# An attention and mixture-of-experts kernel: full and small units of the second expert layer share the code of their first tile

## The chip, the cores and the metric

One core of a Trainium2 chip runs the whole kernel. The metric is the device time of one execution in microseconds; the lower the better. All data is float32; products run on float32 values split into a high and a low part.

## The reference, cut to what matters

Three stages follow one another: pooled attention, a first expert layer with one expert, and a second layer with eight experts. Only the second layer is changed:

```python
N, D, E, F = (2304, 512, 8, 1024)
logits = xn @ en.T / tau                 # xn, en: rows scaled to length 1
expert_idx = np.argmax(logits, axis=1)
gate_w = probs[np.arange(N), expert_idx]
for e in range(E):
    mask = expert_idx == e
    if not mask.any():
        continue
    h = np.maximum(x[mask] @ w1[e], 0.0)
    out[mask] = gate_w[mask, None] * (h @ w2[e])
```

Each row of x goes to one expert, so how many rows an expert has is known only at run time.

## The kernel before

The second layer is class `Moe2`. The rows of each expert are cut into units of 256 (two tiles of 128); up to 17 units are in the program, written out one after the other, and from unit 9 on each stands inside a condition that there are that many. With these inputs units 0 to 11 run. A unit whose rows fit in one tile is small: bit u of `half` is set for it, and it takes another path.

For unit u the program first calls `nxt(u + 1)` (L1298): `gather` (L1187) loads the records of the next unit with a DMA from SyncE's queue (L1195), then gathers its rows with two indirect DMAs from GpSimd's queue (L1205) and drains that queue (L1191); then four loads of the next unit's w1 go to SyncE's queue (`load("1")`, L1167; they move data only where the expert changes).

Then comes the branch on `half` (L1320), taken by every engine for itself. The **full** path: `hidden(f)` for f = 0 to 7 (L1226), 12 products of 256 columns each into a PSUM bank, evicted by ScalarE (L1235) and VectorE (L1236) into `hh` and `hl`; beside each, `split("2", f)` splits one eighth of w2 (ScalarE copy L1172, VectorE subtraction L1173). `load("2")` then queues the next w2. `outer(0, f)` for f = 0 to 7 (L1264) is the second product of the first tile, three products of 512 columns for each f (L1269), all in one bank. Behind f = 0 `x_t` (L1220) transposes the next unit's gathered rows (eight transposes, L1212; copies L1216, subtractions L1217), and behind each f `split("1", f)` splits an eighth of the next unit's w1. `store(rec, 0)` (L1273) scales the bank on ScalarE (L1276) and scatters the rows from GpSimd's queue (L1277). `outer(1, f)` and `store(rec, 1)` do the second tile.

The **small** path: `half(x)` (L1238) makes the first product of one tile the other way round, 2 x 12 products of 512 columns (L1247), with the w2 splits between them, evicts each half as `g` (L1252), and `turn(0)`, `turn(1)` (L1255) transpose each half (L1259) and evict it into `hh`, `hl`. Then `outer(0, f)` for the one tile, with `turn(1)` behind f = 1, `x_t` behind f = 5, a w1 split behind each f, and one store. There is no second tile.

All scatters write the same tensor `out`, so a store on GpSimd's queue waits until the one before it has landed. Engines run their instructions in program order; there is no scheduler that would reorder them here. Where a path is not taken, the program raises the counters (semaphores) by what the other path would have raised, so that later waits hold in either case.

Buffers that matter: banks `d_ph` (3), `d_pt` (2), `d_po` (3, one for each call of `po`), gathered rows `d_xg` (4), outgoing rows `d_ob` (4).

Of the kernel before, what the change touches and what calls it, by code (L numbers as in the profile page):

```python
# [1110 lines left out]
class Moe2:  # L1111
# [150 lines left out]
        nc.vector.tensor_sub(out=l, in0=p, in1=h.bitcast(F32))  # L1262

    def outer(self, t, f):  # L1264
        if f == 0:
            self.o = self.po()
        s = slice(t * 128, t * 128 + 128)
        for q, (a, b) in enumerate(((0, "2h"), (0, "2l"), (1, "2h"))):
            self.nc.tensor.matmul(self.o, lhsT=(self.hh, self.hl)[a][f // 4][:, f % 4, s],  # L1269
                                  rhs=self.w[b, f // 2][:, f % 2],  # L1270
                                  start=f == 0 and q == 0, stop=f == 7 and q == 2)
# [9 lines left out]
    def run(self, items):  # L1281

        nc, tc, rt = self.nc, self.tc, self.rt
        evs = []
        rec, x = self.rec0, self.xt0

        def routing():
            while evs:
                evs.pop(0)()
            while items:  # L1290
                f = items.popleft()
                if f is None:
                    return
                e = f()
                if e:
                    evs.append(e)

        def nxt(u):  # L1298
            r = self.gather(u)
            e = nc.sync.value_load(rt.u[0:1, u, 1:2], min_val=0, max_val=E - 1)  # L1300
            c = nc.sync.value_load(rt.u[0:1, u, 2:3], min_val=0, max_val=1)
            self.load("1", e, c)
            return r, e, c

        first = []

        def step():
            if next(steps, None):
                first.extend(nxt(1))

        with ExitStack() as ifs:  # L1311
            for u in range(UMAX):
                if u >= UMIN:
                    ifs.enter_context(tc.If(total > u))
                more = u + 1 < UMAX
                if more and u:
                    (rec1, xs1), e, c = nxt(u + 1)
                if u:
                    x1 = (self.xh(), self.xl()) if more else None
                    with tc.If((half & (1 << u)) == 0) as full:  # L1320
                        for f in range(8):
                            self.hidden(f, x)
                            self.split("2", f)
                        if more:
                            self.load("2", e, c)
                        for f in range(8):
                            self.outer(0, f)
                            if more:
                                if f == 0:
                                    self.x_t(xs1, x1)  # L1330
                                self.split("1", f)
                        self.store(rec, 0)
                        for f in range(8):
                            self.outer(1, f)
                        self.store(rec, 1)
                    with full.Else():
                        self.half(x)
                        if more:
                            self.load("2", e, c)
                        for f in range(8):  # L1340
                            self.outer(0, f)
                            if f == 1:
                                self.turn(1)
                            if more:
                                if f == 5:
                                    self.x_t(xs1, x1)
                                self.split("1", f)
                        self.store(rec, 0)
                    x = x1
                else:  # L1350
                    for f in range(2, 8):
                        self.hidden(f, x)
                        routing()
                        if f == 4:
                            steps = rt.units()
                        for _ in range(min(3, f - 3)):
                            if not first:
                                step()
                        for i in {4: (2, 3), 5: (4, 5), 6: (6, 7)}.get(f, ()):
                            self.split("2", i)  # L1360
                    for f in range(8):
                        self.outer(0, f)
                        step()
                    self.store(rec, 0)
                    self.load("2", *first[1:])
                    for f in range(6):
                        self.outer(1, f)
                        step()
                    while not next(steps, 1):
                        pass  # L1370
                    (rec1, xs1), e, c = first
                    for f in (0, 2, 4, 6):
                        self.split("1", f)
                    x = self.xh(), self.xl()
                    self.x_t(xs1, x, lambda: self.outer(1, 6))
                    self.outer(1, 7)
                    total = nc.values_load(rt.u[0:1, 0, 2:3], min_val=UMIN, max_val=UMAX)
                    half = nc.values_load(rt.half[0:1, 0:1], min_val=0, max_val=(1 << (UMAX + 1)) - 1)
                    for f in (1, 3, 5, 7):
                        self.split("1", f)  # L1380
                    self.store(rec, 1)
                if more:
                    rec = rec1
# [135 lines left out]
```

## Time and profile before

| what | value |
|---|---|
| median of 3 runs | 1192.37 us (1190.85 to 1193.21) |
| profiled execution, its own time | 1190.95 us |
| its span, first to last instruction | 1189.1 us |
| TensorE products busy, share of the span | 1145.3 us, 96% |
| VectorE, ScalarE, GpSimd busy | 882.1, 740.6, 600.4 us |
| mean granted clock of TensorE | 0.987 |
| second layer, unit 1 to the end | from 950.4 us |

The table is an average over three stages; the rows below are of the second layer alone. Times in them are microseconds from the start of the span; "[2.22 <-X]" is idle time of the engine ahead of the row and what by the profile ended it. A TensorE row is drawn to the modelled end of its last product, so it overlaps the next one a little. PEld is the weight load that goes with each product, PEldq its instruction queue (branches, counters).

### The profile page before, as it was taken

To read this page: it belongs to the slowest core of one execution; us is meant where nothing else is said; L and a number is where in the kernel's file an instruction comes from. 1 tells how busy PE (TensorE), PEld (TensorE's weight loads), DVE (VectorE), ACT (ScalarE), POOL (GpSimd) and SP (SyncE) were. 2 spreads that over 40 slices of the span, in tenths; PEclk is the share of its full clock that TensorE was granted. 3 is DMA by queue.
4 is the path that set the end of the run, shared out by engine and by line. 5 is a ranking of instruction groups with operands and counts; after the bars stand their busy time and mean duration, and the time that the engine had idled before them with its cause. 6 is when DMAs were issued, how large, how long until landed. Compare 5 with 4: busy or idle time off the path is not lost. (4 is left out here: it accounts for less than half of the span.)

```text
span 1189.1 us, 21181 instructions
## 1 busy us (share of the span) xinstructions
PE 1145.3 (96%) x7315; PEld 1064.7 (90%) x7315; DVE 882.1 (74%) x1593; ACT 740.6 (62%) x1451; POOL 600.4 (50%) x525
## 2 busy tenths in 40 slices
PE   7999999999999999799789999999999999999997
PEld 6999999999999999689679988998889899887886
DVE  6888898899999998698845674565455776666775
ACT  5888888878788787344334445444435466666664
POOL 6998988877888872698950222012110221121211
PEclk9999999999999999899989999999999999999999
DMA  7787777785869754555314211111222121286443
GB/s 186 176 191 175 173 183 172 167 204 141 208 151 214 169 124 122 162 168 165 123 46 124 72 46 66 55 54 32 78 89 93 46 72 37 77 267 210 141 144 131
DMA packets 87189, 156.14 MB, mean 131 GB/s; under 512 B 26871, under 2 KB 44279, under 8 KB 87056
## 3 DMA queue, kind: packets, MB, share of 16 engines
q1 hardware_dynamic: 82352, 142.34, 44.7%
q0 software_dynamic: 4336, 11.58, 2.9%
q8 instruction: 67, 1.10, 0.4%
q10 hardware_dynamic: 368, 0.59, 0.2%
q14 instruction: 66, 0.54, 0.2%
HBM read 145.84 MB, written 20.08 MB: 140 GB/s over the span
## 5 line engine op out<-in xcount | busy, mean ns | idle before, releaser
L235 DVE TENSOR_SCALAR_CACHE_REDUCE e<-sc 128x1152 f32<-128x1152 f32 x144 | 194.7, 1352 | 23.5 <-PE sc L231 22.2
L242 ACT ACTIVATE e<-e,nm 128x1152 f32<-128x1152 f32 x144 | 183.7, 1276 | 4.8 <-DVE e L235 4.8
L231 PE MATMUL sc<-kT,qt 128*128 128x384 f32 x780 | 159.0, 339 | 9.8 <-DVE e L235 8.2
L269 ACT CAST pth<-pa 128x768 fp32r<-128x768 f32 (+2 forms) x160 | 116.3, 737 | 80.5 <-PE pa L260 80.5
L271 DVE TENSOR_TENSOR ptl<-pa,pth 128x768 fp32r<-128x768 f32 (+2 forms) x160 | 138.9, 876 | 19.9 <-ACT pth L269 7.7
L1173 DVE TENSOR_TENSOR e<-e,e 128x512 fp32r<-128x512 f32 x200 | 129.4, 687 | 30.2 <-ACT e L1172 14.2
L582 DVE SCALAR_TENSOR_TENSOR u<-h,u 128x320 f32<-128x320 f32 (+1 forms) x112 | 55.8, 498 | 128.8 <-ACT u L581 128.2
L578 ACT ACTIVATE u<-h,half 128x320 f32<-128x320 f32 (+1 forms) x112 | 59.8, 534 | 142.7 <-PE h L563 134.3
L231 PEld LDWEIGHTS sc<-kT,qt 128*128 128x128 f32 x780 | 132.2, 188 | 12.3 <-DVE e L235 9.6
L1269 PE MATMUL d_po<-e,e 128*128 128x512 f32 x504 | 120.9, 393 | 0.0
L260 PE MATMUL pa<-idf,e 128*128 128x128 f32 x864 | 117.6, 272 | 1.7 <-DVE ptl L271 1.7
L595 PE MATMUL y<-wh,gl 128*128 128x512 f32 x288 | 113.9, 395 | 0.8 <-POOL gl L586 0.8
L1172 ACT CAST e<-e 128x512 fp32r<-128x512 f32 x200 | 113.7, 619 | 0.7 <-issue 0.3
L595 PE MATMUL y<-wh,gh 128*128 128x512 f32 x288 | 113.9, 395 | 0.0
L595 PE MATMUL y<-wl,gh 128*128 128x512 f32 x288 | 113.6, 394 | 0.0
L1277 POOL DMA_INDIRECT out<-d_ob,d_rec x19 | 22.1, 1162 | 176.9 <-ACT d_ob L1276 120.5
L1269 PEld LDWEIGHTS d_po<-e,e 128*128 128x128 f32 x504 | 92.6, 188 | 18.6 <-DVE e L1173 0.3
L260 PEld LDWEIGHTS pa<-idf,e 128*128 128x128 f32 x864 | 102.9, 140 | 7.0 <-DVE ptl L271 1.3
L563 PE MATMUL h<-xth,wh 128*128 128x320 f32 (+1 forms) x448 | 90.8, 325 | 16.5 <-POOL wh L57 9.5
L584 ACT CAST gh<-u 128x320 fp32r<-128x320 f32 (+1 forms) x112 | 52.4, 468 | 84.9 <-DVE u L582 84.9
L535 POOL TENSOR_TENSOR xl<-xth,xl 128x512 f32<-128x512 f32 (+1 forms) x14 | 18.3, 1306 | 168.6 <-DMA xl<-av_b 139.9
L285 PE MATMUL av<-pth,vh 128*128 128x288 f32 x576 | 103.2, 306 | 0.0
(257 smaller groups left out, 2639.0 us busy)
## 6 DMA issues: line engine op xcount, KB each, us to landing
e<-moe_w SPq DMA_DIRECT2D x104, 512.0 KB
kr<-k SPq DMA_DIRECT2D x63, 288.0 KB
qr<-q SPq DMA_DIRECT2D x62, 288.0 KB
kk<-kT SPq DMA_DIRECT2D x60, 288.0 KB
vr<-v SPq DMA_DIRECT2D x16, 576.0 KB
av_b<-avs SPq DMA_DIRECT2D x64, 128.0 KB
wi<-moe_w_in SPq DMA_DIRECT2D x16, 512.0 KB
wo<-moe_w_out SPq DMA_DIRECT2D x16, 512.0 KB
```

The lines of the kernel that those rows point to most:

```text
L231: nc.tensor.matmul(s[:, j, 0:384], lhsT=a, rhs=b[:, 384 * j:384 * j + 384], start=i == 0, stop=i == len(mm) - 1)
L235: nc.vector.tensor_scalar(out=e.rearrange("p (a b) -> p a b", a=3), in0=s[:, :, 0:384], scalar1=-0.5 / D ** 0.5, scalar2=None, op0=ALU.mul ...
L242: self.nc.scalar.activation(e, e, AF.Exp, bias=d["nm"][:, t:t + 1], scale=-1.0, accum_out=d["sum"][:, t:t + 1])
L260: nc.tensor.transpose(p[:, c // 3, (c % 3) * 128:(c % 3) * 128 + 128], e[:, i * 128:(i + 1) * 128], idf)
L269: nc.scalar.copy(hi, p)
L271: nc.vector.tensor_sub(out=lo, in0=p, in1=hi.bitcast(F32))
L285: nc.tensor.matmul(box["t"][:, 0:GQ], lhsT=self.vh[:, h * 9 + i % 9], rhs=p[:, i % 9, c0:c0 + GQ], start=i == 0, stop=i == 17)
L563: nc.tensor.matmul(ps[:, :n], lhsT=a[:, k], rhs=b[:, k, h0:h0 + n], start=i == 0, stop=i == 11)
L595: self.nc.tensor.matmul(y, lhsT=a, rhs=b, start=j == 0 and q == 0, stop=j == NF - 1 and q == 2)
L1172: self.nc.scalar.copy(hi, r)
L1173: self.nc.vector.tensor_sub(out=lo, in0=r, in1=hi.bitcast(F32))
L1269: self.nc.tensor.matmul(self.o, lhsT=(self.hh, self.hl)[a][f // 4][:, f % 4, s], rhs=self.w[b, f // 2][:, f % 2], start=f == 0 and q == 0, ...
```

## The change

In each unit from 1 on the branch on `half` now holds less. The full path keeps its eight `hidden` and w2 splits, the w2 loads and `outer(0, 0)`, `outer(0, 1)`; the small path keeps `half`, the w2 loads, the same two and `turn(1)`. What follows stands once, for both: `outer(0, 2)` to `outer(0, 7)` with the w1 splits (0 and 1 ahead of f = 2, then f - 1 ahead of each f, 7 at the end), `x_t` ahead of f = 4, and the first store. A second branch on the same bit, without an else path, holds the second tile. The bank of the output is taken outside of the branch, and no longer inside `outer`.

```diff
     def outer(self, t, f):
-        if f == 0:
-            self.o = self.po()
         s = slice(t * 128, t * 128 + 128)
...
                 if u:
                     x1 = (self.xh(), self.xl()) if more else None
+                    self.o = self.po()
                     with tc.If((half & (1 << u)) == 0) as full:
                         for f in range(8):
                             self.hidden(f, x)
                             self.split("2", f)
                         if more:
                             self.load("2", e, c)
-                        for f in range(8):
+                        for f in range(2):
                             self.outer(0, f)
-                            if more:
-                                if f == 0:
-                                    self.x_t(xs1, x1)
-                                self.split("1", f)
-                        self.store(rec, 0)
-                        for f in range(8):
-                            self.outer(1, f)
-                        self.store(rec, 1)
                     with full.Else():
                         self.half(x)
                         if more:
                             self.load("2", e, c)
+                        for f in range(2):
+                            self.outer(0, f)
+                        self.turn(1)
+                    for f in range(2, 8):
+                        if more:
+                            if f == 4:
+                                self.x_t(xs1, x1)
+                            for i in (0, 1) if f == 2 else (f - 1,):
+                                self.split("1", i)
+                        self.outer(0, f)
+                    if more:
+                        self.split("1", 7)
+                    self.store(rec, 0)
+                    with tc.If((half & (1 << u)) == 0):
+                        self.o = self.po()
                         for f in range(8):
-                            self.outer(0, f)
-                            if f == 1:
-                                self.turn(1)
-                            if more:
-                                if f == 5:
-                                    self.x_t(xs1, x1)
-                                self.split("1", f)
-                        self.store(rec, 0)
+                            self.outer(1, f)
+                        self.store(rec, 1)
                     x = x1
```

In unit 0 two calls of `po` are moved out of `outer`, with nothing else changed.

## Rows read from the trace of the kernel before

**Rows 1.** Units 3, 5: length, busy us PE PEld DVE ACT POOL, clock, DMA.

```profile
996.50:1019.60 23.10, 23.10 (x154) 21.16 (x153) 15.04 (x26) 13.76 (x28) 4.34 (x4) 1.00 0.15 48
1042.80:1058.00 15.20, 12.98 (x66) 10.75 (x66) 10.40 (x17) 11.53 (x22) 3.15 (x3) 1.00 0.73 237
```

**Rows 2.** TensorE, units 4 to 6: start, us, line, tiles, count, [idle before].

```profile
1030.96 0.84 PE L1269 MATMUL d_po<-e,e 128*128 128x512 f32 x3
1032.44 10.46 PE L1269 MATMUL d_po<-e,e 128*128 128x512 f32 x45
1045.12 1.16 PE L1247 MATMUL d_ph<-e,d_xh 128*128 128x512 f32 x4 [2.22 <-ACT e L1172]
...
1055.73 1.03 PE L1212 MATMUL d_pt<-idf,d_xg 128*128 128x128 f32 x8
1057.98 0.93 PE L1233 MATMUL d_ph<-d_xh,e 128*128 128x256 f32 x4
```

**Rows 3.** TensorE in order of time, units 7 to 11.

```profile
1083.34 1.32 PE L1247 MATMUL d_ph<-e,d_xh 128*128 128x512 f32 x4 [2.06 <-ACT e L1172]
...
1097.78 0.93 PE L1233 MATMUL d_ph<-d_xh,e 128*128 128x256 f32 x4
...
1121.27 1.08 PE L1247 MATMUL d_ph<-e,d_xh 128*128 128x512 f32 x4
...
1132.97 1.29 PE L1212 MATMUL d_pt<-idf,d_xg 128*128 128x128 f32 x8 [0.98 <-DMA d_xg<-y_rows,d_rec]
...
1135.49 0.87 PE L1233 MATMUL d_ph<-d_xh,e 128*128 128x256 f32 x4
...
1172.24 0.66 PE L1212 MATMUL d_pt<-idf,d_xg 128*128 128x128 f32 x4 [0.85 <-DMA d_xg<-y_rows,d_rec]
```

**Rows 4.** TensorE's branches (L1320), ns min/median/max: at 1039 us, at 1077 us.

```profile
L1320 PEldq COMPARE_BRANCH  x1: 5944/5944/5944, 1039.0 to 1039.0; - x1
L1320 PEldq COMPARE_BRANCH  x2: 315/2946/5576, 1077.1 to 1077.6; - x2
```

**Rows 5.** GpSimd in time: stores, gather (unit 5); gathers (units 7, 9).

```profile
1038.52 1.38 POOL L1277 DMA_INDIRECT out<-d_ob,d_rec  x1 [14.12 <-ACT d_ob L1276]
1047.11 1.00 POOL L1277 DMA_INDIRECT out<-d_ob,d_rec  x1 [7.21 <-DMA out<-d_ob,d_rec]
...
1049.71 1.17 POOL L1205 DMA_INDIRECT d_xg<-y_rows,d_rec  x1 [0.30 <-PE d_pt L1259]
...
1089.31 1.37 POOL L1205 DMA_INDIRECT d_xg<-y_rows,d_rec  x1 [0.30 <-PE d_ph L1247]
...
1128.04 0.97 POOL L1205 DMA_INDIRECT d_xg<-y_rows,d_rec  x1 [0.30 <-issue]
```

**Rows 6.** Issue to landing: store at 1038.52; gathers, units 5, 7, 9.

```profile
DMA to landing us min/median/max: 7.8/7.8/7.8
DMA to landing us min/median/max: 4.0/4.5/5.0
DMA to landing us min/median/max: 3.6/4.1/4.7
DMA to landing us min/median/max: 5.5/5.8/6.2
```

**Rows 7.** ScalarE in order of time, outer products of unit 4.

```profile
1033.24 4.27 ACT L1172 CAST e<-e 128x512 fp32r<-128x512 f32 x8
1037.55 0.69 ACT L1276 ACTIVATE d_ob<-d_po,d_rec 128x512 f32<-128x512 f32 x1
```

**Rows 8.** TensorE: counter step at a skipped block; last products.

```profile
L1311 PEldq EVENT_SEMAPHORE  x1: 51/51/51, 1183.2 to 1183.2; - x1
...
1181.16 1.98 PE L1269 MATMUL d_po<-e,e 128*128 128x512 f32 x8
```

**Rows 9.** TensorE, unit 7: length, busy (instructions), granted clock, DMA share, GB/s.

```profile
1084.20:1087.60 3.40, 3.40 (x10) 0.50 0.55 181
1087.60:1091.00 3.40, 3.40 (x19) 1.00 0.77 264
```

More of the change, by code (lines that the diff above doesn't have):

```diff
@@ L1360, in run @@
                             self.split("2", i)
+                    self.o = self.po()
                     for f in range(8):
@@ L1365, in run @@
                     self.load("2", *first[1:])
+                    self.o = self.po()
                     for f in range(6):
```

## The prediction

> **What bounds the kernel now.** The change touches only the second layer, so I split that by unit. Which units are full and which are small is read from the products: units 1 to 4, 6, 8, 10 and 11 run L1233 (full), units 5, 7 and 9 run L1247 (small); unit 11 is the last one that runs. The first view is the table of stretches: in a full unit TensorE is busy all of its 23.1 us, in a small unit it is not (13.0 of 15.2 us) [rows 1]. Whatever the change brings or costs, it must show as idle TensorE in units 5, 7, 9, or as new idle time in the eight full ones. The second view is TensorE in order of time. There are two kinds of holes. Units 5 and 7 begin with 2.22 and 2.06 us of nothing, unit 9 does not [rows 2, 3]. And the transposes of the next unit's rows wait for their gather: 0.98 us in unit 9 and 0.85 us in unit 11 [rows 3].
>
> The hole at the start of units 5 and 7 is labelled as a wait for a ScalarE copy, but that copy writes w2 parts which the first L1247 products don't read, and w1 was split a unit earlier. The branch instructions explain it: TensorE's branch into the small part took 5944 ns in unit 5 and 5576 ns in unit 7, where the branch at the end of the full part ahead of it took 315 ns [rows 4]. The first started at 1039.0, when the products queued ahead of it still had 3.9 us to run (they end at 1045.12 - 2.22 = 1042.9); the rest is the hole. It looks like code that had to be fetched. The Trainium skill says so ("Runtime: NRT & Kernel Launch", Instruction fetch mechanics): code comes in blocks of 256 instructions, only two are held, and a taken branch to outside of them waits for a fetch. By that rule the trace fits: the full part is 152 products with a weight load each, 304 instructions, so the jump over it can pass a whole block; in the change only 102 products are jumped, 204 instructions, and the target is in this block or the next.
>
> The second chain is GpSimd's queue. The gather for the next unit stands behind the second store of the unit before, which waits until the first store has landed: issued at 1038.52, landed 7.8 us later, so the second store went at 1047.11, and the second gather at 1049.71 [rows 5]. Its rows land 5.0 us after that, at 1054.7; in unit 7 at 1089.31 + 4.7 = 1094.0, in unit 9 at 1128.04 + 5.5 = 1133.5 [rows 5, 6] (the larger of the two numbers is given to the second gather; in unit 9 the other way would fit worse, as the waiting transposes start at 1132.97 [rows 3]). All three lie in stretches where the next expert's weights are loaded.
>
> **The change, part by part.** A product of 512 columns costs 0.23 us (45 in 10.46 us, the last one drawn at full length) [rows 2], the eight transposes of x_t 0.8 us (from 1030.96 + 3 x 0.23 to 1032.44) [rows 2].
>
> Full units: the same products, transposes, splits and stores; no sum on TensorE. x_t moves from behind outer(0, 0) to ahead of outer(0, 4), 9 products or 2.1 us later; its result is first read in the next unit, over 5 us after. ScalarE does three splits of 0.53 us first, then waits for the transposes (1030.96 + 12 x 0.23 + 0.4 = 1034.2), copies until 1035.3, and does five splits until 1038.0; before, it was at 1037.5, with the store at 1037.55 [rows 2, 7]. So the **first store goes 0.5 us later**, and behind it on GpSimd the second store and the gathers. In unit 11 the later x_t finds its rows there: **-0.85 us** [rows 3]. One more taken branch in the middle and one more test: some 0.3 us each in the sequencer [rows 4], hidden by the queued products ahead.
>
> Small units: the hole at the start goes (-2.2, -2.1), the gather does not come sooner, and x_t moves **forward**, from behind outer(0, 5) to ahead of outer(0, 4). In unit 5 x_t began 1055.73 - 1045.12 = 10.6 us after the first product; 6 products fewer lie ahead now, so 9.2 us. It would be due at 1042.9 + 9.2 = 1052.1, in unit 7 at 1081.3 + 9.2 = 1090.5, in unit 9 at 1130.5. The rows land at 1054.7, 1094.0, 1133.5: the saved holes turn into a wait for the gather (a hole that stayed would be over at 1045.1 and x_t due at 1054.3, still ahead of its rows, so the sum hardly hangs on it), and the 6 products that used to run before x_t now stand behind it on TensorE, as do splits 3 to 7 and the store on ScalarE.
>
> A new cost at the end of a small unit: the second tile is a block of its own that is jumped. A jumped block must still raise the counters that its products would have raised; the trace shows such a step once, on TensorE at the end of unit 11: it ran at 1183.2, after the last product's end at 1183.14, and the branch after it took 0.19 us [rows 8]. So TensorE **drains**: product's end 0.16 us past its slot, counter, two branches, test, and a first weight load that nothing covers (about 0.2 us): I take 0.85 us, worked out from these; bounds 0.3 (only the tail of a product) and 1.5.
>
> From the landing on a small unit then needs 0.4 (second transposes) + 12 x 0.23 + 0.85 = 4.0 us. Next unit at 1058.7, 1098.0, 1137.5; before at 1057.98, 1097.78 and 1135.49, with the first four products 0.3 us slow in each (0.93, 0.93, 0.87 for about 0.62) because splits came late, which the drain now covers [rows 2, 3]. Differences: +0.4, -0.1, +1.7, together **+2.0 us**. Later landing: +0.3 per unit of the 0.5 above, **+0.9** (nothing if the store is bound by the loads' bytes anyway, 1.5 at most). In units 5 and 7 the products start 2 us sooner, so two of the w2 loads are issued sooner and stand ahead of the gathers; unit 9, which had no hole, shows the gather at 5.5 us for 5.0 and 4.7: **+0.8 each, 1.6** (0 to 3).
>
> Clock: after the hole of unit 7 the granted clock fell to 0.50 (1.2 GHz) for 3.4 us, in which 10 products ran where 19 run at full clock (2.4 GHz) [rows 9]: 1.7 us. It is inside unit 7's time before. The new waits (2.6, 3.5 and 3.0 us and longer) are longer than that hole, so I count **one such fall in three units, +1.7** (0 to 5.1).
>
> Sum: 2.0 + 0.9 + 1.6 - 0.85 + 1.7 = **+5.3 us**. Against the profiled execution (1190.95, span 1189.1) this is 1196.3; that execution is 1.4 us under the median of the runs shown (1192.37), and I go between the two: **1197**.
>
> **Rivals.** (1) The gathers land as before and the clock stays up: 2.0 - 0.85, about +1.2 us, 1192 to 1193.6. For: the store's landing is set by the four loads issued ahead of it. Against: longer waits than the one that lost the clock. Chance 0.25. (2) **Faster**: the gathers land before x_t is due. Small units then take 9.2 + 0.8 + 2.8 + 0.85 = 13.6 us: units 6, 8 and 10 start at 1056.5, 1094.9 and 1134.9, with the 0.3 -1.8, -3.2 and -0.9, and -0.85 in unit 11: -6.7, some 1185. It decides at a landing 9.2 us after the unit's start, 2.6 to 3.5 us sooner than in the trace. For: it is the landing under load that is slow (7.8 us for the store), and loads could fall otherwise. Against: no issue on GpSimd moves forward. Chance 0.12. (3) Code fetch gets worse: a branch in the middle of each full unit meets missing code. With 6 long and some 12 short products queued ahead (1.4 + 1.3 us) 5.9 us of fetch leaves 3.2, in eight units up to 26 us; 1200 to 1220. The same page of the Trainium skill speaks against further branches in this way; by its block size the jump of some 80 instructions should not leave the two blocks. In the trace the full part's end jump (past the small part's 64 products, 315 ns) never cost a hole. Chance 0.05.
>
> **Numbers.** Forecast 0.58, rivals 0.25, 0.12, 0.05. About 0.2% (2.4 us) is what a measurement can tell from no change. Slower 0.60 (the forecast and rival 3, less the forecast's lowest corner), same 0.27, faster 0.13. The forecast's own range is 1193.5 to 1203 (bounds of landing, drain and clock); with rival 1 from 1191 to 1202.5.
>
> **What would show it.** Right: no TensorE branch over 1 us into units 5, 7, 9 and no hole there; L1212 in those units idle 2.5 to 4.5 us on the gather; an idle stretch of some 0.9 us ahead of units 6, 8 and 10; unit 11 without wait; full units still 23.1 us. Wrong: L1212 of small units without wait (rival 2), holes behind outer(0, 1) of full units (rival 3), or a hole left at the start of unit 5 or 7, which would mean that it was no jump.

## The result, and the profile of the changed kernel

The changed kernel takes 1201.51 us (median), 1.0081 times the kernel before, 95% interval 1.0066 to 1.0096: 9.1 us slower at the medians. One of its five executions took 2100.6 us at a mean granted clock of 0.819; the ratio leaves it out, and without it the median is 1200.61 us. The profiled execution took 1201.92 us with a span of 1200.1, 11.0 us more than the span of before. In this kernel the outer products are L1267, stores L1274 (ScalarE) and L1275 (GpSimd), the first test L1319, the second test L1344 (the two branches on `half`); hidden products L1233, half L1247, turn L1259 and x_t L1212 keep their lines.

TensorE of the changed kernel, units 5 and 6, in order of time (start us, us, engine, line, tiles, shapes, count, in brackets the idle time before and what ended it):

```profile
1041.53 1.08 PE L1247 MATMUL d_ph<-e,d_xh 128*128 128x512 f32 x4
...
1049.20 1.64 PE L1267 MATMUL d_po<-e,e 128*128 128x512 f32 x6
1053.96 0.66 PE L1212 MATMUL d_pt<-idf,d_xg 128*128 128x128 f32 x4 [3.11 <-DMA d_xg<-y_rows,d_rec]
1055.75 1.09 PE L1212 MATMUL d_pt<-idf,d_xg 128*128 128x128 f32 x4 [1.13 <-DMA d_xg<-y_rows,d_rec]
1056.49 5.46 PE L1267 MATMUL d_po<-e,e 128*128 128x512 f32 x12
1062.42 0.73 PE L1233 MATMUL d_ph<-d_xh,e 128*128 128x256 f32 x4 [0.47 <-PEq L1344]
```

The same view, units 7, 9 and 11:

```profile
1085.21 1.08 PE L1247 MATMUL d_ph<-e,d_xh 128*128 128x512 f32 x4
...
1097.35 0.66 PE L1212 MATMUL d_pt<-idf,d_xg 128*128 128x128 f32 x4 [2.82 <-DMA d_xg<-y_rows,d_rec]
1099.37 1.09 PE L1212 MATMUL d_pt<-idf,d_xg 128*128 128x128 f32 x4 [1.37 <-DVE d_xl L1217]
1100.11 4.24 PE L1267 MATMUL d_po<-e,e 128*128 128x512 f32 x12
1104.82 0.73 PE L1233 MATMUL d_ph<-d_xh,e 128*128 128x256 f32 x4 [0.47 <-PEq L1344]
...
1127.61 1.08 PE L1247 MATMUL d_ph<-e,d_xh 128*128 128x512 f32 x4
...
1139.22 0.66 PE L1212 MATMUL d_pt<-idf,d_xg 128*128 128x128 f32 x4 [2.20 <-DMA d_xg<-y_rows,d_rec]
1141.30 1.09 PE L1212 MATMUL d_pt<-idf,d_xg 128*128 128x128 f32 x4 [1.43 <-DVE d_xl L1217]
1142.04 5.36 PE L1267 MATMUL d_po<-e,e 128*128 128x512 f32 x12
1147.95 0.73 PE L1233 MATMUL d_ph<-d_xh,e 128*128 128x256 f32 x4 [0.56 <-PEq L1344]
...
1185.18 1.03 PE L1212 MATMUL d_pt<-idf,d_xg 128*128 128x128 f32 x8
```

Four things are to be read, each against its row of before. The holes (idle time of TensorE) of 2.22 and 2.06 us at the heads of units 5 and 7 [rows 2, 3] are gone. In all three small units x_t now waits, twice: once for each of its two tiles. (The second wait of units 7 and 9 is labelled as a VectorE subtraction; the second gather was issued at 1093.30 and landed 5.9 us later, at 1099.2, which fits the 1099.37 at which the transposes began.) The 12 products behind x_t take 4.2 to 5.5 us, where 0.23 us each would make 2.8. And each small unit ends with half a microsecond in which TensorE's sequencer is at the second test. Unit 11 no longer waits (0.85 us before, [rows 3]).

Why the 12 products are slow is in the table of stretches (length, then busy us and instructions of PE, PEld, DVE, ACT, POOL, then the granted clock, the DMA share and GB/s), taken over the stretches of low clock:

```profile
1054.99:1061.80 6.81, 6.05 (x16) 4.56 (x16) 4.39 (x7) 3.42 (x7) 0.00 (x0) 0.50 0.51 165
1099.37:1102.76 3.39, 3.39 (x10) 2.88 (x11) 1.65 (x3) 2.26 (x5) 0.00 (x0) 0.50 0.00 0
1140.33:1147.13 6.80, 5.83 (x16) 4.56 (x16) 4.39 (x7) 3.34 (x7) 0.00 (x0) 0.50 0.02 5
```

A granted clock of 0.50 (1.2 GHz) stands behind each of the three waits, for 17.0 us in all; before, it was once, for 3.4 us [rows 9].

TensorE's branch at the first test, at the three changes from a full to a small unit (ns min/median/max, then the time):

```profile
L1319 PEldq COMPARE_BRANCH  x1: 218/218/218, 1037.8 to 1037.8; - x1
L1319 PEldq COMPARE_BRANCH  x1: 438/438/438, 1081.5 to 1081.5; - x1
L1319 PEldq COMPARE_BRANCH  x1: 430/430/430, 1124.0 to 1124.0; - x1
```

The 5944 and 5576 ns of before [rows 4] are not there. What the long branches wait for is in the same traces. In the kernel before, one packet of instructions runs on DMA queue 8 from 1040 to 1044 us, inside the branch of 5944 ns (queue, packets, MB, share of 16 engines):

```profile
q8 instruction: 1, 0.02, 1.6%
```

It is 16 KB, runs from 1042.41 to 1043.44 us, and the branch ends 1.5 us behind it. In the 13 traces of this case TensorE has 20 branches of over 1 us; each has one such packet in it, which ends 1.4 to 1.5 us ahead of the branch's end, and no branch of under 1 us into a small unit has one. So the holes are a wait for code, which the prediction could only infer. Last, GpSimd around unit 5 (first store of unit 4, its second store, second gather for unit 6), and the time from issue to landing of that first store and of the gathers:

```profile
1037.66 1.27 POOL L1275 DMA_INDIRECT out<-d_ob,d_rec  x1 [14.43 <-ACT d_ob L1274]
1047.10 1.00 POOL L1275 DMA_INDIRECT out<-d_ob,d_rec  x1 [8.17 <-ACT e L1261]
...
1049.69 0.97 POOL L1205 DMA_INDIRECT d_xg<-y_rows,d_rec  x1 [0.30 <-PE d_pt L1259]
...
DMA to landing us min/median/max: 8.6/8.6/8.6
DMA to landing us min/median/max: 5.5/5.7/5.9
```

The first store goes 3.87 us ahead of the unit's start; before, 4.38 (1038.52 against 1042.90) [rows 5]. It takes 8.6 us to land for 7.8, and the gather 5.9 for 5.0 [rows 6]. So the second gather is issued 8.2 us behind the unit's start for 6.8, and its rows land 14.1 us behind it for 11.8; the transposes of its tile begin at 14.2. Unit 9 is alike (issued at 8.1 for 6.8). In unit 7 the issue is hardly later (8.1 for 8.0), and it is the landing that takes longer, 5.9 us for 4.7 [rows 6].

The whole in one table: lengths of the units in us from the first product of one to the first of the next (the code wait at the head of units 5 and 7, where there is one, is counted to them), and the time at a granted clock of 0.50 ahead of the last product. The rows below the second are the experiments of the next section.

```
kernel                        u5     u6     u7     u8     u9    u10   at 0.50
before                      15.08  23.30  16.50  23.49  14.22  23.32    3.4
changed                     20.89  22.79  19.61  22.79  20.34  23.20   17.0
changed, second profile     19.28  23.20  18.19  22.79  18.02  22.78   10.2
x_t ahead of outer(0, 6)    16.83  22.79  17.93  22.80  14.85  23.22    3.4
x_t behind the first store  14.30  23.78  14.31  23.38  14.40  23.38    0
old branches, x_t forward   17.03  23.63  16.62  23.48  17.91  23.07   10.2
work in the wait            19.90  22.78  17.71  23.20  20.68  22.79    6.8
work at the head            17.08  23.20  16.48  23.20  17.14  22.78    0
gathers between the stores  13.37  23.26  13.37  23.26  13.59  22.79    0
gathers two ahead           13.35  23.30  13.36  22.93  13.60  22.79    0
old branches, two ahead     15.26  23.24  14.96  23.08  13.48  23.08    0
```

Each row is one profiled execution, and not all of these are near their kernel's median: the changed kernel's second profile took 1198.34 us (median 1201.52), x_t behind the first store 1186.22 (1188.14), work at the head 1191.78 (1195.62), old branches with gathers two ahead 1188.41 (1189.72), and work in the wait 1200.32 (1196.23).

In the changed kernel the three small units are 5.8, 3.1 and 6.1 us longer, 15.0 together. The units behind them are 1.3 us shorter, unit 11 1.1 us; the rest of the difference to 11.0 lies ahead of unit 1 (-1.2), in units 1 to 4 (-0.2) and in the last stores (-0.3).

### The profile page after: what moved, and what is told of

It reads as the page before. It is cut to its first block, busy times and chain, and to the rows that moved or that the text cites. A ratio compares the mean times of both kernels' runs of the same rounds, so it can differ in the third digit from the quotient of the medians.

```text
span 1200.1 us, 21374 instructions
## 1 busy us (share of the span) xinstructions
PE 1151.2 (96%) x7315; PEld 1068.8 (89%) x7315; DVE 880.1 (73%) x1593; ACT 739.2 (62%) x1451; POOL 598.6 (50%) x525
## 5 line engine op out<-in xcount | busy, mean ns | idle before, releaser
L1267 PE MATMUL d_po<-e,e 128*128 128x512 f32 x504 | 127.1, 407 | 0.3 <-DVE e L1173 0.3
L1275 POOL DMA_INDIRECT out<-d_ob,d_rec x19 | 21.2, 1118 | 191.2 <-ACT d_ob L1274 126.0
L1267 PEld LDWEIGHTS d_po<-e,e 128*128 128x128 f32 x504 | 96.9, 197 | 20.5 <-DVE e L1173 0.8
```

## The experiments

The theory: a small unit is bound by the landing of the next unit's rows and by what stands behind x_t on TensorE; the branches that the change mends were covered by that wait; the wait then costs more than its length, through the clock. The main rival: the branch structure itself, with its second test, is what costs.

**The changed kernel again**, as a yardstick for the runs beside it.

> The changed kernel once more, unedited, beside the three others of this group, so that they can be compared on one chip. Theory: the loss is a property of the program and not of one execution: 1.008 of the kernel before, about 1201 us, with the waits on the gather in units 5, 7 and 9. Rival: part of the loss was chance in the landings of the first profile, then 1.004 or less, 1196 us.

Measured: 1.0066 (1.0044 to 1.0088), 1201.52 us. The loss is the program's. Its profile, one execution of 1196.6 us span, differs from the first in size: the clock was low for 3.4 us behind each of the three waits, and the transposes of the second gather's rows began 13.9, 13.1 and 12.5 us behind the units' starts, for 14.2, 14.2 and 13.7. Nothing in the program differs, so up to 1.2 us of landing and 1.7 us of clock per unit (half of 6.8 - 3.4) vary from execution to execution.

**x_t later in the new structure.**

```diff
                         if more:
-                            if f == 4:
+                            if f == 6:
                                 self.x_t(xs1, x1)
```

> The changed kernel with one edit: in the shared products x_t stands ahead of outer(0, 6), where the small units had it before the change, not ahead of outer(0, 4). Theory: a small unit is bound by the landing of the next rows (14.2, 14.2 and 13.7 us after its start in the changed kernel) plus everything that stands behind x_t on TensorE. Six products (6 x 0.23 = 1.4 us at full clock, 2.7 at half) move out from behind that wait in each of units 5, 7, 9, so at least 3 x 1.4 = 4.2 us are saved, and up to 11.8 if the granted clock also stays up (units of about 16.5 us in place of 20.9, 19.6, 20.3): 1189.7 to 1197.3 us. Rival: the 9 us come from the branch structure (the second test with its drained TensorE, the branches), and x_t's place is of no matter: 1201 us, as the changed kernel.

Measured: 1.0015 (1.0000 to 1.0030), 1192.98 us. Some 6 to 8 us of the 9 are gone with six products moved, and structure and second test are all still there: the rival falls. The transposes of the second gather's rows still begin 14.3, 14.1 and 12.2 us behind the units' starts, x_t still waits (6.6 us in five waits), but less stands behind it and the clock falls once only.

**The old structure with x_t forward.** The branches of before, x_t ahead of outer(0, 4) in both parts (the small part is shown, the full part is edited alike):

```diff
                         for f in range(8):
+                            if more and f > 1:
+                                if f == 4:
+                                    self.x_t(xs1, x1)
+                                for i in (0, 1) if f == 2 else (f - 1,):
+                                    self.split("1", i)
                             self.outer(0, f)
                             if f == 1:
                                 self.turn(1)
-                            if more:
-                                if f == 5:
-                                    self.x_t(xs1, x1)
-                                self.split("1", f)
+                        if more:
+                            self.split("1", 7)
                         self.store(rec, 0)
```

> The other half of the change alone: the branches of the kernel before (each kind of unit has its products in a part of its own, no second test), but x_t ahead of outer(0, 4) and the splits in the order of the change, in both parts. Theory: x_t's place does most of the harm. The holes at the start of units 5 and 7 come back (2.2 and 2.1 us), but they run beside the gather's way, so the units still end at the landing plus 0.4 + 12 products; no drain (about 0.5 us each). With a clock that falls as in the changed kernel about 1198 to 1201, with less of it 1195. TensorE's branch into units 5 and 7 over 5 us again, and a wait on the gather in all three. Rival: the shared structure is what costs; then this runs as the kernel before, 1192.

Measured: 1.0027 (1.0009 to 1.0046), 1195.33 us. The holes are back (2.82 and 2.16 us, TensorE's branch into unit 5 takes 6544 ns), and as TensorE comes later to x_t, it waits less there (1.1 us at most, 3.1 in the changed kernel). Old branches and late x_t 1, new branches 1.0015, forward x_t 1.0027, both 1.007 to 1.008: the two edits together cost more than their sum. The theory's wording "x_t's place does most of the harm" is thus too strong: x_t forward costs 3 us with the old branches and 6 to 8 with the new, where no hole stands ahead of it. Not all of the 3 us is x_t's: of the 10.2 us at half clock one fall of 3.4 us stands at the hole of unit 5 and one at that of unit 7, the third behind x_t's waits in unit 9, and before had only the one at unit 7 (a fall of 3.4 us costs 1.7 at most). Unit 9 has 0.91 us of idle TensorE behind its first four products, which neither side said; it comes again (0.52 us) in the old kernel below that gathers two units ahead. In both a packet of instructions ends 1.4 and 1.3 us ahead of the product that ends the idle time (1125.54 for 1126.94, 1121.89 for 1123.22), as in the holes. That fits a wait for code behind a short branch; no run tests it.

**Work at the head of a small unit**, where before had its hole.

```diff
                     with full.Else():
+                        p = self.ph()
+                        for j in range(9):
+                            nc.tensor.matmul(p, lhsT=x[0][:, 0, 0:128], rhs=self.w["1h", 0][:, 0],
+                                             start=j == 0, stop=j == 8)
                         self.half(x)
```

> The changed kernel with work added: nine products (2.1 us) at the head of a small unit, into a PSUM tile that nothing reads, in the place of the hole that the kernel before had there. Theory of the prediction: the hole was cover, since the gather's way runs beside it. Then the added 2.1 us come off the wait of x_t (2.0 to 3.1 us) and cost nothing, and as the clock falls for less time the kernel is 3 to 6 us faster than the changed one: 1195 to 1198 us. If, besides, the w2 loads that stand ahead of the gathers in the changed kernel (the term of 0.8 us per unit) are behind them again, the second gather lands within 13.0 us of the unit's start in units 5 and 7 (13.7 and 13.7 in the changed kernel, 13.3 and 12.5 in its second profile): 1193 us. Rival: the nine products push all that follows, the gather's way included, and cost their whole 6.2 us: 1206 us or more.

Measured: 1.0028 (1.0014 to 1.0042), 1195.62 us: with 27 useless products the kernel is 5 us faster than without them. TensorE in unit 5 (L1330 is the added work):

```profile
1040.93 2.22 PE L1330 MATMUL d_ph<-e,d_xh 128*128 128x512 f32 x9
...
1052.24 0.66 PE L1212 MATMUL d_pt<-idf,d_xg 128*128 128x128 f32 x4
1054.22 0.63 PE L1212 MATMUL d_pt<-idf,d_xg 128*128 128x128 f32 x4 [1.32 <-DMA d_xg<-y_rows,d_rec]
1054.60 2.99 PE L1267 MATMUL d_po<-e,e 128*128 128x512 f32 x12
1058.01 0.73 PE L1233 MATMUL d_ph<-d_xh,e 128*128 128x256 f32 x4 [0.42 <-PEq L1348]
```

The first wait is gone, the 12 products take 2.99 us, and in this execution the clock stays at 1.00 in all small units. That execution is 3.8 us under the median, and the six of the ten executions that took over 1195 us have a mean granted clock of 0.986 to 0.991, for 0.992 here, so the clock may well have fallen in those. The rows are released to TensorE 13.3, 12.7 and 13.2 us behind the units' starts (the expectation counts to the last packet, about half a microsecond less: 12.6 and 12.2 in units 5 and 7). That is sooner than in the first profile of the changed kernel and 39.2 us in sum, as the 39.5 of the second: the hole was cover, which is shown. Whether the w2 loads ahead of the gathers cost what the prediction gave them is not shown; the time is 1195.6, not the 1193 that went with it.

**Work in the wait itself.**

```diff
                         self.turn(1)
+                        p = self.ph()
+                        for j in range(10):
+                            nc.tensor.matmul(p, lhsT=self.hh[0][:, 0, 0:128], rhs=self.w["2h", 0][:, 0],
+                                             start=j == 0, stop=j == 9)
```

> The changed kernel with work added: ten more products (2.3 us) behind the second turn of a small unit, into a PSUM tile that nothing reads, which fill most of the wait for the gather (3.1, 2.8 and 2.2 us). Theory: part of the loss is the granted clock, which falls to 0.50 after these waits for 6.8, 3.4 and 6.8 us (12 products in 5.46, 4.24 and 5.36 us in place of 2.8). If the idle stretch is the reason, filling it keeps the clock up and the kernel gets faster with more work in it: -2.5, -1.3 and -2.4 us, about 1195 to 1196 us. The second hole, between the two transposes (1.1 to 1.4 us), stays and may cost a part of this: up to 1199. Rival: the clock falls whatever stands in the wait, then 1201 (or up to 1202 where ten products are longer than the wait).

Measured: 1.0036 (1.0020 to 1.0052), 1196.23 us. The stretches of low clock (columns as above) are two:

```profile
1056.78:1060.17 3.39, 3.11 (x10) 2.66 (x11) 1.60 (x4) 1.99 (x4) 0.00 (x0) 0.50 0.48 160
1142.11:1145.50 3.39, 3.39 (x10) 2.61 (x9) 2.96 (x5) 2.99 (x6) 0.00 (x0) 0.50 0.01 2
```

6.8 us in all, for 17.0 and 10.2 in the two profiles of the changed kernel. In unit 7, where two idle pieces of 0.90 and 0.76 us were left, the clock did not fall; in units 5 (0.91 and 1.40) and 9 (2.12 and 0.71) it did. The ratio is 0.3% to 0.5% lower than the changed kernel's two (its interval overlaps with that of the second by a little), some 4 to 5 us with 30 products more, as the theory has it; in this one profile the units are no shorter than in the second of the changed kernel, as the rows came later (14.5, 13.9 and 15.2 us behind the starts). The cleaner case is the one ahead: there no wait over 1.4 us is left in the small units, and in its profile the clock doesn't fall in the second layer's units. So part of the change's loss is not the wait but what the wait does to the products behind it; how much, this run alone does not say.

**x_t behind the first store.**

```diff
                         if more:
-                            if f == 4:
-                                self.x_t(xs1, x1)
                             for i in (0, 1) if f == 2 else (f - 1,):
...
                     self.store(rec, 0)
+                    if more:
+                        self.x_t(xs1, x1)
                     with tc.If((half & (1 << u)) == 0):
```

> The changed kernel with x_t behind the first store, ahead of the second test, so that all eight of the shared outer steps are done before TensorE waits for the next rows. Theory: after the landing only the second transposes (0.4), the ScalarE copy (0.6) and the start of the next unit are left, for 0.4 + 6 x 0.23 + drain where x_t stands ahead of outer(0, 6): about 1 us less per small unit than that kernel, 1189 to 1191 us, if the clock stays up; the wait on the gather nearly vanishes in unit 9. Rival: what the later place saves on TensorE it loses in the evacuation of the last tile (copy 0.6, subtract 0.7) that the next unit's products wait for: 1193 us as with x_t ahead of outer(0, 6), or more.

Measured: 0.9956 (0.9938 to 0.9974), 1188.14 us: faster than before by 5 us, and better than the theory said, for a reason that it did not have. GpSimd around unit 5 (first store of unit 4, second gather), then TensorE:

```profile
1036.82 1.02 POOL L1275 DMA_INDIRECT out<-d_ob,d_rec  x1 [13.18 <-ACT d_ob L1274]
...
1047.94 0.97 POOL L1205 DMA_INDIRECT d_xg<-y_rows,d_rec  x1 [0.30 <-issue]
```

```profile
1053.81 1.13 PE L1212 MATMUL d_pt<-idf,d_xg 128*128 128x128 f32 x8
1056.24 0.73 PE L1233 MATMUL d_ph<-d_xh,e 128*128 128x256 f32 x4 [1.31 <-ACTq L1344]
```

The unit starts at 1041.94. The first store of the full unit ahead is issued 5.12 us before that, not 3.87, since ScalarE no longer evacuates x_t ahead of it; the second gather goes at +6.0 for +8.2. x_t begins at +11.9 without idle time, and the transposes of the second gather's rows at +12.3, for +14.2. So x_t's place in the *full* unit sets when the store, and behind it the gathers, are issued: 1.25 us sooner at the store became 1.9 us at the rows in unit 5, 1.7 and 1.3 in units 7 and 9. Against the second profile of the changed kernel it is only 1.6, 0.6 and 0.1. The price is 1.31 us at the end of the unit, where the evacuation has no products beside it.

**The gathers between the two stores.**

```diff
+        early = {}
+
         def nxt(u):
-            r = self.gather(u)
+            r = early.pop(u, None) or self.gather(u)
...
                     self.store(rec, 0)
+                    if u + 2 < UMAX:
+                        early[u + 2] = self.gather(u + 2)
                     with tc.If((half & (1 << u)) == 0):
```

> The changed kernel with one edit: the gather of the rows of unit u+2 is issued in unit u between its first and its second store, not behind the second. Theory: the second store waits for the landing of the first, and this is what makes the gathers late. They would then be issued some 9 us sooner, behind the w1 loads but ahead of the w2 loads, land some 6 us after the start of a small unit, and x_t (due 9.3 us after it) waits for nothing; no idle stretch, so no fall of the clock there. Small units of 9.3 + 0.8 + 2.8 + 0.5 = 13.4 us for 20.9, 19.6, 20.3: about 1181 us. Rival 1: the landing is set by the bytes of the loads on the queues, not by the moment of issue: the wait stays above 2 us per unit, 1197 to 1201. Rival 2: the second store, now behind the gathers and their drain, comes so late that the next unit's first store waits: faster than the changed kernel, but by less, 1186 to 1192.

Measured: 0.9961 (0.9944 to 0.9977), 1185.98 us. Small units of 13.37, 13.37 and 13.59 us, as worked out, no wait of x_t in them, no fall of the clock. GpSimd around unit 5, and at the end of the kernel:

```profile
1039.82 1.26 POOL L1275 DMA_INDIRECT out<-d_ob,d_rec  x1 [13.37 <-ACT d_ob L1274]
1041.38 0.99 POOL L1205 DMA_INDIRECT d_xg<-y_rows,d_rec  x1 [0.30 <-PE d_po L1267]
...
1050.02 1.24 POOL L1275 DMA_INDIRECT out<-d_ob,d_rec  x1 [6.38 <-ACT e L1172]
...
1181.46 1.02 POOL L1275 DMA_INDIRECT out<-d_ob,d_rec  x1 [5.10 <-ACTq L1311]
```

5 us of the expected 20 did not come, and 4 of them are at the end: in the last unit a gather that nothing needs stands between the stores, and the last store goes 4.1 us behind the end of its ScalarE copy (1177.35), for 0.3 in the changed kernel. That is the mechanism of the second rival, but at one place only; in unit 5 the first store (1058.23) goes 0.3 us behind its copy and waits for nothing. The first rival falls.

**The gathers two units ahead, in the new and in the old kernel.** At the head of a unit the rows of the unit after the next are gathered; the order of stores and gathers stays.

```diff
-        self.rec = Ring(p, 3, [128, 2, 4], U32, "d_rec")
+        self.rec = Ring(p, 4, [128, 2, 4], U32, "d_rec")
...
+        early = {}
+
         def nxt(u):
-            r = self.gather(u)
+            r = early.pop(u, None) or self.gather(u)
+            if 2 <= u < UMAX - 1:
+                early[u + 1] = self.gather(u + 1)
```

> The changed kernel with the gathers one unit further ahead: at the head of unit u the rows of unit u+2 are gathered, those of u+1 have been gathered a unit before (one more buffer of records). GpSimd's order of stores and gathers stays, only what is gathered is a unit younger. Theory: no x_t waits any more, the stores are not held up by a gather that stands between them, and the last unit's second store is not late (4.3 us in the kernel with the gathers between the stores): small units of 13.4 us, 1181 to 1183 us. Rival: the gathers were in fact held up by the loads and now hold the loads up in turn (w1 and w2 late, splits late, holes of 1 us or more ahead of the next unit's products): 1186 us or more.

> The kernel before with the same edit, gathers one unit further ahead. With the gather out of the way this and its counterpart differ by the change alone. Theory: the holes at the starts of units 5 and 7 stay (2.2 and 2.1 us, TensorE's branches of over 5 us), and so do the late splits in the units behind; only the two waits on the gather go (0.98 and 0.85 us): 1188.5 to 1191 us, so that the change is worth 5 to 8 us once the rows are there. Rival: the holes came from what the gather delayed, not from the branch; then they go too, and both kernels are within 1 us of each other at 1182 to 1184.

Measured, new: 0.9911 (0.9882 to 0.9939), 1184.05 us; old: 0.9974 (0.9951 to 0.9997), 1189.72 us. TensorE at unit 5 with the new structure:

```profile
1051.94 1.64 PE L1267 MATMUL d_po<-e,e 128*128 128x512 f32 x6
1053.42 1.03 PE L1212 MATMUL d_pt<-idf,d_xg 128*128 128x128 f32 x8
1054.21 2.98 PE L1267 MATMUL d_po<-e,e 128*128 128x512 f32 x12
1057.60 0.73 PE L1233 MATMUL d_ph<-d_xh,e 128*128 128x256 f32 x4 [0.42 <-ACT e L1172]
```

and with the old one, with TensorE's two branches at the test there, the longer of them into the small part:

```profile
1046.54 1.17 PE L1247 MATMUL d_ph<-e,d_xh 128*128 128x512 f32 x4 [2.38 <-ACT e L1172]
...
L1324 PEldq COMPARE_BRANCH  x2: 174/3137/6100, 1039.9 to 1040.3; - x2
```

With the rows there in time, the holes stay in the old kernel (2.38 and 2.07 us) and between the two kernels the change is now worth 0.5% to 0.6%, about 6 us: its gain is real, and it was the gather that ate it. The rivals of both runs fall. The new kernel with this edit is 0.9% faster than the kernel before; run a second time, beside the next kernel, it was at 0.9922:

> The kernel with the gathers two units ahead once more, beside the one made longer, and for a tighter interval: 0.989 to 0.994 of the kernel before, 1181 to 1185 us, small units of 13.4 us and no branch over 1 us into them.

Measured: 0.9922 (0.9905 to 0.9939), 1182.93 us, small units of 13.35, 13.36 and 13.59 us, branches of 437 ns at most into them.

**A longer jump.** The same kernel, with useless transposes in the full part:

```diff
                             self.outer(0, f)
+                        for _ in range(13):
+                            p = self.pt()
+                            for k in range(4):
+                                nc.tensor.transpose(p[:, k], self.cn["idf"], self.cn["idf"])
                     with full.Else():
```

> The kernel with the gathers two units ahead, with the full part made longer: 52 transposes of the identity, which nothing reads, at its end. A small unit jumps over 154 products and transposes in place of 102 (the kernel before: 152). Theory: the length of the jump made TensorE wait for code. Then the branch into units 5 and 7 takes over 5 us again and these units begin with a hole of 1.5 to 3 us, with no change in gathers, stores or loads of a small unit. The transposes themselves add about 0.07 us each, some 3.7 us in each of eight full units, 30 us in all: about 1219 us, of which 4 to 5 are the holes. Rival: the hole belonged to the old parts' other differences (the second tile inside, the work behind it); then no branch into a small unit is over 1 us and there is no hole.

Measured: 1.0317 (1.0296 to 1.0338), 1229.09 us; the transposes took 5.7 us per full unit, not 3.7, which with 1183 makes the time. TensorE's branches at the first test around the starts of units 5, 7 (two in that stretch) and 9, and unit 5's first products:

```profile
L1323 PEldq COMPARE_BRANCH  x1: 5167/5167/5167, 1060.9 to 1060.9; - x1
L1323 PEldq COMPARE_BRANCH  x2: 301/318/335, 1095.9 to 1104.6; - x2
L1323 PEldq COMPARE_BRANCH  x1: 362/362/362, 1146.8 to 1146.8; - x1
...
1066.25 1.16 PE L1247 MATMUL d_ph<-e,d_xh 128*128 128x512 f32 x4 [1.44 <-ACT e L1172]
```

The hole is back in unit 5, and in units 7 and 9 it is not. So a longer jump can bring the wait for code, which no shorter jump here did; but its length does not decide alone, since jumps of the same length cost 5167, at most 335, and 362 ns. The first has an instruction packet in it (from 1063.25 to 1064.63 us), the other two have none. By the Trainium skill ("Runtime: NRT & Kernel Launch", Instruction fetch mechanics) code is refilled in whole blocks of 256 instructions; then where a jump lies in them should matter too. That would fit the three values, and the kernel before, where unit 9 had no hole. No run here moved the place of a jump alone.

## Why the prediction was right, and where its sum was off

Direction and range held: slower, 1201.5 for 1197 in 1191 to 1202.5. The sum was +5.3 us against the profiled execution, which came out at +11.0. So the mechanism was right and two sizes were not, and that the time still lies inside the range, by 1.0 us, is in part luck: what else was off went the other way, 2.6 us in sum. By its steps:

- **The holes go and turn into a wait.** Right. Branches of 218 to 438 ns, no hole, x_t waiting 2.2 to 3.1 us; and the holes were code, as the instruction packets in the long branches show. That a hole left standing would cost nothing is shown by the work put in its place: 6.2 us of it made the kernel faster.
- **x_t forward leaves 12 products behind the landing.** Right. Six of them moved ahead again took back 6 to 8 us.
- **Later landing (+0.9) and w2 loads ahead of the gathers (+1.6).** The second gather landed 2.3, 1.3 and 1.3 us later than before, counted from the units' starts (4.9 in sum), in the second profile 2.0, 0.2 and 0.1 (2.3), for 2.5 predicted: half of it in the one execution, about right in the other. The store did go 0.5 us later, as said. But I priced the landing as passing that on at 0.3 per unit; in unit 5 the store also took longer to land, and 0.5 us became 1.4 at the gather's issue (8.16 for 6.81), while in unit 7 the gather was issued as before and landed later. With the store moved 1.25 us the other way the rows came 1.3 to 1.9 us sooner than in the first profile, 0.1 to 1.6 sooner than in the second. How much the w2 loads have of it is not settled.
- **The drain (0.85 each).** Too high by itself: 0.47, 0.47 and 0.56 us idle ahead of units 6, 8 and 10. The step that it is a part of, from the landing to the next unit, was right: it took 19.2 us in the three units, 7.6 of them by the low clock, which leaves 3.9 a unit for 4.0. What the drain was over, the other parts were under (the 12 products take 2.99 us at full clock, for 2.76).
- **One fall of the clock (+1.7).** This is the term that was mis-sized. The clock fell in all three small units, for 17.0 us in the first profile and 10.2 in the second, in which TensorE was busy for 15.3 and 9.8 us: 7.6 and 4.9 us lost at the half clock. I had seen it fall after a hole of 2.06 us and took the new, longer waits for one fall in three; the rows gave no reason for the third. The bound of 5.1 that I kept for the range was nearer to both, and would have made the sum 8.7.
- **Unit 11 (-0.85).** Right: its wait is gone, the unit is 1.1 us shorter.

The difference of 5.7 us in the sum is thus 5.9 from the clock and 2.4 from the landing, less 0.4 from the drain and what stands around it, and less 2.2 elsewhere: 1.2 of it ahead of unit 1, where the change does nothing, the rest in units 1 to 4, the units behind the small ones, unit 11 and the last stores, each 0.5 or less.

Of the rivals, the first (gathers as before, clock up) fell on the clock. The second (the rows there before x_t is due) did not happen, but the runs with earlier gathers are its test: small units of 13.4 us, worked out as 13.6, and a kernel faster than before by 9 to 10 us where no gather stands late at the end. The third (a branch in the middle of full units that waits for code) did not happen: units 1 to 4 are 23.1 us long as before.

## What to carry to other kernels

Before a stall is taken away, look at what runs beside it: a hole ahead of a wait is cover for what the wait is for, and its price is what is left when that is taken off. When code is shared between two kinds of work, look where each shared step lay in each of them; moving a step that waits ahead of steps that don't costs them all. Price a new idle stretch of TensorE with the products behind it at half clock, and, if the fix is to fetch earlier, put the fetch ahead by a whole unit of work, and not between two stores of which the second is the last thing that the kernel does.

## What the runs showed of the hardware

- The granted clock fell to 0.50 (1.2 GHz) behind each of the six waits of 2.0 to 3.1 us, with a second one of 0.3 to 1.5 us close behind, in the two profiles of the changed kernel, and stayed there for 3.4 or 6.8 us. How long the wait was does not settle it alone: holes of 2.22 us (before), 2.38 and 2.07 us (old branches, two ahead) had no fall behind them, holes of 2.06 us (before), 2.82 and 2.16 us (old branches, x_t forward) had one of 3.4 us. 27 useless products at the heads of the small units made the kernel faster, by 0.4% to 0.5%.
- The same program, profiled twice, had the rows of a small unit 0.3 to 1.2 us apart and the low clock for 17.0 and 10.2 us: one profile's sum of such terms is not good to better than some 5 us here.
- An indirect store issued 0.5 us later against its unit landed 1.3 us later in unit 5 (8.6 us from issue for 7.8) and 0.1 us later in unit 7 (8.6 for 9.0); one issued 1.25 us sooner brought what waited for it 2.2 us sooner (the second gather at +6.0 for +8.2).
- Jumps over the same number of instructions cost TensorE 5167, at most 335, and 362 ns. In each of the 20 branches of over 1 us in these traces a packet of 16 KB on the instruction queue ends 1.4 to 1.5 us ahead of the branch's end.
